# Half products in two bank tiles, with the last product's matmuls between them, and weight differences in later slots

## The chip, the cores and the metric

One core of a Trainium2 chip. The metric is the device time of one execution in microseconds (us); the kernel before takes 1305.6 us in the median of three runs.

## What is computed

Three parts in a chain, all in fp32. The attention is local: chunks of 32 queries with a window of 16 keys to the left and 8 to the right and 8 memory keys, for 4 batches, 8 heads, 768 tokens, head size 64. Then two feed-forward parts over 3072 tokens of width 512:

```python
x = attention(q, k, v, mem_k, mem_v)          # 3072 x 512
h = x @ w_in                                  # 512 x 2048
x = np.where(h > 0, h, np.exp(np.minimum(h, 0)) - 1) @ w_out
a = x @ w1                                    # 512 x 1024
b = x @ w2
out = ((a * b) @ w3) @ w_out2                 # 1024 x 1024, 1024 x 512
```

## The kernel before

Every fp32 operand of a matmul is split into a high and a low part (`split`, `hi_of` and `lo_of`: a cast on ScalarE, a subtraction on VectorE), and a product is three matmuls: high by high, high by low, low by high (`mm3`, and lines 661 to 663 of `mm_half`). The weights come as 64-bit numbers and are put together by `rebase`, `shift` and `low`.

The order of the work is written out by hand: each engine runs its instructions in the order in which the Python code emits them, and a dependency tracker adds the waits. It tracks PSUM and SBUF by tile.

**The middle stage** (the loop over `n` at line 746, blocks of 384 tokens, 16 steps a block). A step runs `mm_h` (12 matmuls, x @ w_in), the activation on ScalarE and VectorE (`elu_exp`, `elu_max` on line 545, `elu_hi` on line 549, `elu_lo` on line 553), and `mm_x` of two steps earlier (12 matmuls with w_out). Between these, `at_step` runs small pieces of other work twice a step, taken from a table of slots that line 500 fills: the attention of the block that comes next, one group of 128 tokens at a time, and the preparation of the second feed-forward part's weights. A `Duo` takes one column block of w1 and w2, forms differences of its parts for the products of the last stage, splits them and stores them to DRAM: `duo_plain`, `duo_first`, `duo_second` and `duo_last`, each into a tile of the pool `st`, which has two buffers. `duo_second` has three subtractions on VectorE (lines 459 to 461, all recorded as line 443) before its cast (line 438) and its last subtraction (line 439). There are eight Duos, two a block in four blocks. `at_out` (slot 8; lines 120 and 121) reads the attention's result out of the PSUM tile `PA`, called `banks` in the trace; `mid_flip` (slot 9) transposes a w3 block into the same tile (line 419) and splits it from there (lines 172 and 175). `store_next` starts the stores of finished tiles at the beginning of each slot.

**The last stage** (the loop at line 848, 32 steps: four pairs of 384-token blocks, times 8 column blocks f of the second part). `mm_ab` computes the columns of a and b for both blocks of a pair in a seven-product scheme of Strassen's kind: seven half products of six matmuls with 384 columns. They alternate between the two banks y and z of `PA`:

```python
    def mm_ab(n):
        y, z = PA[:, 0, 0:TB], PA[:, 1, 0:TB]
```

After a half product ScalarE copies the bank out (lines 669, 673, 675) or VectorE adds it to an earlier result (line 443); the last two give a * b for the two blocks (c11 * c12 and y * c22), which are split into `gq`. Then `left_step` prepares an operand for the next pair, SP issues the loads of weights for step n + 3 (`load_wq`, four loads, 1.8 MB), and `mm_o(n - 1)` multiplies the step before with the folded weights of w3 @ w_out2: 18 matmuls of 512 columns into six accumulators, `PS[0]` to `PS[5]`. Each eighth step is followed by `store_out`, six copies (lines 115 and 117) and six stores.

Of the kernel before, what the change touches and what calls it, by code (L numbers as in the profile page):

```python
# [8 lines left out]
F32 = mybir.dt.float32  # L9
# [10 lines left out]
def tile_kernel(  # L20
# [23 lines left out]
    nc = tc.nc  # L44
    P = 128
# [11 lines left out]
    KT = DM // P  # L57
    NT = B * S
    TB = 384
    NB = NT // TB  # L60
    GPB = TB // GQ
    FF1 = w_in.shape[1] // P
    FF2 = w1.shape[1] // P
# [12 lines left out]
    f_p = ctx.enter_context(tc.tile_pool(name="f_p", bufs=4))  # L76
# [7 lines left out]
    PA = psum.tile([P, 2, 512], F32, name="banks")  # L84
    PS = [None if i < KT else psum.tile([P, 512], F32, name=f"bank{i}") for i in range(6)]
# [27 lines left out]
    def copy_on(eng, o, i):  # L113
        if eng == "a":
            nc.scalar.copy(o, i)
        else:
            nc.vector.tensor_copy(o, i)

    def split(hi, lo, src):
        nc.scalar.copy(hi, src)  # L120
        nc.vector.tensor_tensor(out=lo, in0=src, in1=hi.bitcast(F32), op=ALU.subtract)  # L121

    def mm3(o, w_hi, w_lo, x_hi, x_lo, start, stop):
        mm(o, lhsT=w_hi, rhs=x_hi, start=start, stop=False)  # L124
        mm(o, lhsT=w_hi, rhs=x_lo, start=False, stop=False)  # L125
        mm(o, lhsT=w_lo, rhs=x_hi, start=False, stop=stop)  # L126
# [60 lines left out]
    class Feed:  # L187
# [11 lines left out]
        def do(self, i, *ops):  # L199
            if 0 <= i < len(self.jobs):  # L200
                for op in ops:
                    op(self.jobs[i])
# [239 lines left out]
    def sub(o, a, b, op=ALU.subtract):  # L442
        nc.vector.tensor_tensor(out=o, in0=a, in1=b, op=op)  # L443
        return o
# [39 lines left out]
    def put(at, fn, arg):  # L484
        slots.setdefault(int(at), []).append((at, len(slots.get(int(at), ())), fn, arg))

    def base(G):
        return 2 * FF1 * (G - GPB) // GPB + 1, "slow"
# [6 lines left out]
    def plan(s0, job, *steps):  # L495
        mid_jobs.append(job)
        for at, fn in steps:
            put(s0 + at, fn, job)

    for G in range(GPB, NG):  # L500
        s0, pace = base(G)
        for at, fn in zip(paces[pace], chain):
            put(s0 + at, fn, G)
        if G < GM:
            continue
        if G % GPB and duos:
            duo = duos.pop(0)
            plan(s0, duo.jobs[0], (0, rebase), (1, mid_low))
            plan(s0, duo.jobs[1], (2, rebase), (3, mid_low))
            for at, fn in ((2, duo_plain), (6, duo_first), (7, duo_second), (8, duo_last)):  # L510
                put(s0 + at, fn, duo)
        elif wos:
            plan(s0, wos.pop(0), (0, rebase), (1, mid_low), (2, mid_split))
        if w3s and (not G % GPB or len(duos) % 4 < 3):
            plan(s0, w3s.pop(0), (4, rebase), (5, mid_low), (9, mid_flip))
# [101 lines left out]
    def load_wq(n, parts=range(4)):  # L617
        if n < NPAIR * FF2:
            for r in parts:
                nc.sync.dma_start(out=wq[n % FOLD][r].bitcast(F32), in_=wqd[n % FF2][r])  # L620

    NPAIR = NB // 2
    PLACE = dict(b11=(0, 0), b21=(0, 1), t1=(1, 0), t3=(1, 1), t2=(2, 0), t4=(2, 1), b22=(3, 0))

    def right(n, what):
        r, h = PLACE[what]
        return [wq[n % FOLD][r][:, i, h * 256:(h + 1) * 256] for i in range(2)]
# [5 lines left out]
    def load_x1(p):  # L633
        for r in range(2):
            for k in range(2):
                t = late.tile([P, 2, TB], F32, tag=f"x1{r}{k}", name="x1")
                nc.sync.dma_start(out=t, in_=x1d[2 * p + r][:, 2 * k:2 * k + 2, :])
                x1_t[p, r, k] = t

    def left_step(p, i):  # L640
        a11, a12, a21, a22 = (x1_t[p, r, k] for r in range(2) for k in range(2))
        if i == 3:
            x1_t[p, "s1"] = sub(late.tile([P, 2, TB], F32, tag="s1", name="s1"), a21, a22, ALU.add)
        s1 = x1_t.get((p, "s1"))
        if i == 4:
            sub(a21, a11, a21)
            sub(a11, s1, a11)
        if i == 6:
            sub(a12, a12, a11)
        src = (a11, a12, a22, s1, a11, a21, a12)[i]  # L650
        hi, lo = left[p % 2][LEFTS[i]]
        split(hi, lo, src)

    e_f, gq = {}, []

    def mm_half(n, o, x, w, start, more):
        xs, ws = left[n // FF2 % 2][x], right(n, w)
        for i in range(2):
            c = slice(i * P, (i + 1) * P)
            args = ws[0][:, c], ws[1][:, c], xs[0][:, i, :], xs[1][:, i, :]  # L660
            mm(o, lhsT=args[0], rhs=args[2], start=start and i == 0, stop=False, skip_group_check=more)  # L661
            mm(o, lhsT=args[0], rhs=args[3], start=False, stop=False, skip_group_check=more)  # L662
            mm(o, lhsT=args[1], rhs=args[2], start=False, stop=i == 1, skip_group_check=more)  # L663

    def mm_ab(n):
        y, z = PA[:, 0, 0:TB], PA[:, 1, 0:TB]
        r1, r2, r5, c11, c12, c22 = (e_f[i] for i in range(6))
        mm_half(n, y, "a11", "b11", True, True)
        nc.scalar.copy(r1, y)
        mm_half(n, z, "a12", "b21", True, True)  # L670
        sub(c11, z, r1, ALU.add)
        mm_half(n, y, "s2", "t2", False, True)
        nc.scalar.copy(r2, y)
        mm_half(n, z, "s1", "t1", True, True)
        nc.scalar.copy(r5, z)
        mm_half(n, y, "s3", "t3", False, True)
        sub(c22, y, r5, ALU.add)
        mm_half(n, z, "s4", "b22", False, True)
        sub(c12, z, r2, ALU.add)
        mm_half(n, y, "a22", "t4", False, True)  # L680
        sub(c11, c11, c12, ALU.mult)
        sub(c22, y, c22, ALU.mult)
        for r, e in enumerate((c11, c22)):
            nc.scalar.copy(gq[2 * (n % 2) + r][:, 0, :], e)  # L684
        for r, e in enumerate((c11, c22)):
            g = gq[2 * (n % 2) + r]
            sub(g[:, 1, :], e, g[:, 0, :].bitcast(F32))

    def mm_o(n):
        f = n % FF2  # L690
        w = W[s_wc[f]]
        for t in range(2 * TB // P):
            g = gq[2 * (n % 2) + t // GPB]
            c = slice(t % GPB * P, (t % GPB + 1) * P)
            mm3(PS[t], g[:, 0, c], g[:, 1, c], w[:, 0, :], w[:, 1, :], f == 0, f == FF2 - 1)

    def store_out(p):
        for t in range(2 * TB // P):
            o = f_p.tile([P, 512], F32, tag="f", name="st")
            copy_on("av"[t % 2], o, PS[t])  # L700
            r0 = 2 * p * TB + t * P
            nc.sync.dma_start(out=out[r0:r0 + P, :], in_=o)


    with tc.manual_schedule():
# [40 lines left out]
        for n in range(NH + 2):  # L746
            j, f, at, last = seq[n] if n < NH else (NB, n - NH, n - NH, False)
# [99 lines left out]
        NA = NPAIR * FF2  # L847
        for n in range(NA + 1):
            p, f = divmod(n, FF2)
            if n < NA:  # L850
                mm_ab(n)
                if p + 1 < NPAIR and f >= 1:
                    left_step(p + 1, f - 1)
                if p + 2 < NPAIR and f == FF2 - 1:
                    load_x1(p + 2)
                load_wq(n + FOLD)
            if n >= 1:
                mm_o(n - 1)
                if f == 0:
                    store_out(p - 1)  # L860


# [28 lines left out]
```

## Time and profile before

| | |
|---|---|
| median of three runs | 1305.6 us (1304.9 to 1306.8) |
| profiled execution: its own time | 1306.04 us |
| its span in the trace | 1304.1 us |
| mean granted TensorE clock | 0.98 of full |
| attention and middle stage | up to some 710 us |
| weight products (w3 @ w_out2) | some 708 to 754 us |
| last stage | some 754 to 1300 us |

Engines in the profile: PE is TensorE's matmuls, PEld its weight loads, DVE VectorE, ACT ScalarE, SP the engine that issues nearly all DMAs. A row of the view in order of time gives the start, the duration, engine, line, operation, output <- inputs and, in brackets, how long the engine stood idle before it and who released it. The ends of matmuls are modelled, and they overlap: the pace is read from their starts.

### The profile page before, as it was taken

How to read it: one execution, taken by the hardware profiler on the slowest of the kernel's cores; microseconds unless marked ns; L12 is line 12 of the kernel's file. 1: busy time of each engine (PE TensorE's matmuls, PEld its weight loads, DVE VectorE, ACT ScalarE, POOL GpSimd, SP SyncE). 2: the span in 40 equal slices, each digit the busy share in tenths (PEclk: the TensorE clock that was granted, in tenths of full speed). 3: DMA queues.
4: the chain of work that ended last, by engine and by line, in shares of the span. 5: the costliest groups of instructions: out<-in, count | busy, mean ns of one | idle time of the engine just before them, and what ended most of it. 6: DMA issues, size and time to landing. Idle time of an engine off the chain costs nothing.

```text
span 1304.1 us, 20830 instructions
## 1 busy us (share of the span) xinstructions
PE 1113.8 (85%) x8528; PEld 991.5 (76%) x8528; DVE 596.9 (46%) x1080; ACT 463.1 (36%) x965; POOL 1.7 (0%) x16
## 2 busy tenths in 40 slices
PE   4788998998989989999999977777777777777777
PEld 3788998988989889999999756666666666665665
DVE  4898565665665656654524132233233322322222
ACT  3676454544544545445433121112111211111111
POOL 0000000000000000000000000000000000000000
PEclk9889998998999989999999999999999999999999
DMA  8855554554445545342276343326333543334311
GB/s 205 246 149 130 157 155 152 151 155 160 128 155 150 173 153 152 106 135 69 85 270 195 129 131 112 108 86 226 113 104 106 194 129 112 100 103 161 101 37 49
DMA packets 170090, 180.40 MB, mean 138 GB/s; under 512 B 101388, under 2 KB 140300, under 8 KB 169996
## 3 DMA queue, kind: packets, MB, share of 16 engines
q1 hardware_dynamic: 168956, 178.81, 44.5%
q8 instruction: 67, 1.10, 0.4%
q10 hardware_dynamic: 1040, 0.26, 0.1%
q14 instruction: 27, 0.22, 0.1%
HBM read 139.20 MB, written 39.85 MB: 137 GB/s over the span
## 4 chain that ended last, share of the span: by engine, by line
PE 53%; DVE 22%; ACT 16%; issue 5%; DMA 3%; DVEq 0%; ACTq 0%; SPq 0%
PE banks L661 10%; PE bank L124 9%; PE bank L125 9%; PE bank L126 9%; PE banks L663 6%; PE banks L662 6%; DVE e L443 4%; ACT g L549 3%; DVE eg L545 2%; DVE pT L377 2%; DVE e L366 2%; DVE f L167 1%; DVE g L553 1%; DVE f L163 1%; ACT eg L540 1%
## 5 line engine op out<-in xcount | busy, mean ns | idle before, releaser
L124 PE MATMUL bank<-xhl,w 128*128 128x384 f32 x512 | 179.5, 351 | 13.1 <-DVE eg L545 12.2
L124 PE MATMUL bank<-g,w 128*128 128x384 f32 x512 | 178.8, 349 | 0.0
L125 PE MATMUL bank<-g,w 128*128 128x384 f32 x512 | 174.7, 341 | 0.0
L126 PE MATMUL bank<-g,w 128*128 128x384 f32 x512 | 174.6, 341 | 0.0
L125 PE MATMUL bank<-xhl,w 128*128 128x384 f32 x512 | 173.6, 339 | 0.9 <-DVE xhl L121 0.9
L126 PE MATMUL bank<-xhl,w 128*128 128x384 f32 x512 | 173.5, 339 | 0.0
L661 PE MATMUL banks<-xd,w 128*128 128x384 f32 x224 | 85.7, 383 | 63.2 <-DVE e L443 33.2
L443 DVE TENSOR_TENSOR e<-banks,e 128x384 f32<-128x384 f32 x64 | 35.7, 558 | 195.8 <-PE banks L663 195.8
L549 ACT CAST g<-eg 128x384 fp32r<-128x384 f32 x128 | 66.0, 516 | 160.5 <-DVE eg L545 160.5
L553 DVE TENSOR_TENSOR g<-eg,g 128x384 fp32r<-128x384 f32 x128 | 71.4, 558 | 97.1 <-ACT g L549 97.1
L661 PEld LDWEIGHTS banks<-xd,w 128*128 128x128 f32 x224 | 41.9, 187 | 94.8 <-DVE e L443 48.8
L124 PEld LDWEIGHTS bank<-xhl,w 128*128 128x128 f32 x512 | 97.7, 191 | 20.4 <-DVE eg L545 17.1
L443 DVE TENSOR_TENSOR e<-banks,eg 128x384 f32<-128x384 f32 x64 | 35.7, 558 | 159.9 <-PE banks L663 159.9
L124 PEld LDWEIGHTS bank<-g,w 128*128 128x128 f32 x512 | 98.9, 193 | 1.1
L125 PEld LDWEIGHTS bank<-g,w 128*128 128x128 f32 x512 | 98.8, 193 | 0.2 <-DVE g L553 0.2
L125 PEld LDWEIGHTS bank<-xhl,w 128*128 128x128 f32 x512 | 97.9, 191 | 1.3 <-DVE xhl L121 1.3
L126 PEld LDWEIGHTS bank<-g,w 128*128 128x128 f32 x512 | 98.7, 193 | 0.0
L126 PEld LDWEIGHTS bank<-xhl,w 128*128 128x128 f32 x512 | 97.8, 191 | 0.0
L545 DVE SCALAR_TENSOR_TENSOR eg<-eg,bank 128x384 f32<-128x384 f32 x128 | 69.8, 545 | 60.4 <-ACT eg L540 60.4
L684 ACT CAST g<-e 128x384 fp32r<-128x384 f32 x64 | 32.9, 513 | 175.8 <-DVE e L443 175.8
L539 ACT ACTIVATE eg<-bank 128x384 f32<-128x384 f32 x128 | 62.5, 489 | 61.5 <-PE bank L126 61.5
L663 PE MATMUL banks<-xd,w 128*128 128x384 f32 x224 | 75.6, 338 | 0.0
(135 smaller groups left out, 1910.9 us busy)
## 6 DMA issues: line engine op xcount, KB each, us to landing
w<-wqd SPq DMA_DIRECT2D x96, 512.0 KB
raw<-in_moe_w_dram SPq DMA_DIRECT2D x32, 512.0 KB
wqd<-st SPq DMA_DIRECT2D x24, 512.0 KB
raw<-in_moe_w_out_dram SPq DMA_DIRECT2D x20, 512.0 KB
w3d<-st SPq DMA_DIRECT2D x16, 512.0 KB
w<-w3d SPq DMA_DIRECT2D x16, 512.0 KB
w<-wqd SPq DMA_DIRECT2D x32, 256.0 KB
raw<-in_moe_w_in_dram SPq DMA_DIRECT2D x12, 512.0 KB
```

The source lines that it names most:

```text
L124: mm(o, lhsT=w_hi, rhs=x_hi, start=start, stop=False)
L125: mm(o, lhsT=w_hi, rhs=x_lo, start=False, stop=False)
L126: mm(o, lhsT=w_lo, rhs=x_hi, start=False, stop=stop)
L443: nc.vector.tensor_tensor(out=o, in0=a, in1=b, op=op)
L539: nc.scalar.activation(e, h_t[n], AF.Relu, scale=-1.0)
L545: nc.vector.scalar_tensor_tensor(out=e, in0=e, scalar=-1.0, in1=h_t.pop(n), op0=ALU.add, op1=ALU.max)
L549: nc.scalar.copy(g_t[n][:, 0, :], eg_t[n])
L553: nc.vector.tensor_tensor(out=g[:, 1, :], in0=eg_t.pop(n), in1=g[:, 0, :].bitcast(F32), op=ALU.subtract)
L661: mm(o, lhsT=args[0], rhs=args[2], start=start and i == 0, stop=False, skip_group_check=more)
L662: mm(o, lhsT=args[0], rhs=args[3], start=False, stop=False, skip_group_check=more)
L663: mm(o, lhsT=args[1], rhs=args[2], start=False, stop=i == 1, skip_group_check=more)
L684: nc.scalar.copy(gq[2 * (n % 2) + r][:, 0, :], e)
```

## The change

Half products go into `PS[4]` and `PS[5]`, two tiles of one bank each. The last product's accumulators five and six go into the two halves of `PA`, which is one tile. The 18 matmuls of the last product no longer follow the step as a block: they stand in six groups of three between its half products, after the second, third, fourth and fifth (one group each) and after the seventh (two). `left_step` is issued ahead of the first group, and the copy and the store of an accumulator directly behind its group. In the middle stage the slots of the weight differences change: `duo_first` from 6 to 7, `duo_last` from 8 (ahead of what the group of attention does later) to 8.5, `duo_second` from 7 to 9.5.

```diff
-            for at, fn in ((2, duo_plain), (6, duo_first), (7, duo_second), (8, duo_last)):
+            for at, fn in ((2, duo_plain), (7, duo_first), (8.5, duo_last), (9.5, duo_second)):
...
+    def acc(t):
+        return PS[t] if t < KT else PA[:, t - KT, :]
+
+    def mm_step(n, last, between):
+
+        y, z = PS[4][:, 0:TB], PS[5][:, 0:TB]
+        if last:
+            for i in sorted(between):
+                between[i]()
+            return
         r1, r2, r5, c11, c12, c22 = (e_f[i] for i in range(6))
+        do = lambda i: between[i]() if i in between else None
         mm_half(n, y, "a11", "b11", True, True)
         nc.scalar.copy(r1, y)
         mm_half(n, z, "a12", "b21", True, True)
         sub(c11, z, r1, ALU.add)
+        do(0)
         mm_half(n, y, "s2", "t2", False, True)
         nc.scalar.copy(r2, y)
+        do(1)
         mm_half(n, z, "s1", "t1", True, True)
         nc.scalar.copy(r5, z)
+        do(2)
         mm_half(n, y, "s3", "t3", False, True)
         sub(c22, y, r5, ALU.add)
+        do(3)
         mm_half(n, z, "s4", "b22", False, True)
         sub(c12, z, r2, ALU.add)
         mm_half(n, y, "a22", "t4", False, True)
+        do(4)
+        do(5)
         sub(c11, c11, c12, ALU.mult)
         sub(c22, y, c22, ALU.mult)
...
+    def mm_o(n, t):
...
+    def store_out(p, t):
...
         for n in range(NA + 1):
             p, f = divmod(n, FF2)
+
+            def behind(t, n=n, p=p, f=f):
+                if t == 0 and n < NA and p + 1 < NPAIR and f >= 1:
+                    left_step(p + 1, f - 1)
+                if n >= 1:
+                    mm_o(n - 1, t)
+                    if f == 0:
+                        store_out(p - 1, t)
+
+            mm_step(n, n == NA, {t: lambda t=t: behind(t) for t in range(2 * GPB)})
             if n < NA:
...
                 load_wq(n + FOLD)
-            if n >= 1:
-                mm_o(n - 1)
-                if f == 0:
-                    store_out(p - 1)
```

What the change does to the issue order, at three places. First PE, in the second step of the last stage, about the second half product; `banks` is the tile `PA`, `bank_95` and `bank_96` are `PS[4]` and `PS[5]`, `bank_606` is `PS[0]`, and what a row waits for stands in brackets. Before, the first half, the second half and the start of the third:

```order
L661 MATMUL banks<-xhl_73,w_77 128x384
L662 MATMUL banks<-xhl_73,w_77 128x384
L663 MATMUL banks<-xhl_73,w_77 128x384
L661 MATMUL banks<-xhl_73,w_77 128x384 [waits Activation_49]
L662 MATMUL banks<-xhl_73,w_77 128x384
L663 MATMUL banks<-xhl_73,w_77 128x384
L661 MATMUL banks<-xhl_73,w_77 128x384
L662 MATMUL banks<-xhl_73,w_77 128x384
L663 MATMUL banks<-xhl_73,w_77 128x384
L661 MATMUL banks<-xc_7195,w_79 128x384 [waits DMAHW6_49,DVE_49]
```

And now, from the end of the second half on:

```order
L663 MATMUL bank_96<-xhl_73,w_77 128x384
L661 MATMUL bank_96<-xhl_73,w_77 128x384
L662 MATMUL bank_96<-xhl_73,w_77 128x384
L663 MATMUL bank_96<-xhl_73,w_77 128x384
L124 MATMUL bank_606<-w_76,g 128x512 [waits Activation_49]
L125 MATMUL bank_606<-w_76,g 128x512
L126 MATMUL bank_606<-w_76,g 128x512 [waits DVE_49]
L661 MATMUL bank_95<-xc_7195,w_79 128x384 [waits DMAHW6_49,Activation_49]
L662 MATMUL bank_95<-xc_7195,w_79 128x384
```

The second half has lost its wait for ScalarE (Activation); the last product's first group stands between the second and the third half, and the third half waits for ScalarE, which reads the first.

Second, VectorE in the middle stage, in the last group of attention of a block with weight differences; line 377 belongs to the attention, 443 and 439 to the weight differences (`duo_first`, then `duo_second`, and a single 439 of `duo_last`), 545 and 553 to the activation, 121 to `at_out`, 175 to `mid_flip`. Before:

```order
L377 STREAM_TRANSPOSE pT<-e_3386 128x1024
L443 TENSOR_TENSOR st<-f 128x256 x2
L439 TENSOR_TENSOR st<-st 128x512
L443 TENSOR_TENSOR st<-f 128x256
L443 TENSOR_TENSOR st<-st,f 128x256
L443 TENSOR_TENSOR st<-f,st 128x256
L439 TENSOR_TENSOR st<-st 128x512
L545 SCALAR_TENSOR_TENSOR eg<-eg,bank_95 128x384
L553 TENSOR_TENSOR g<-eg,g 128x384
L121 TENSOR_TENSOR xhl_74<-banks,xhl_74 128x2x4x64
L439 TENSOR_TENSOR st<-f,st 128x256
L175 TENSOR_TENSOR st<-banks,st 128x512
```

And now:

```order
L377 STREAM_TRANSPOSE pT<-e_3386 128x1024
L443 TENSOR_TENSOR st<-f 128x256 x2
L439 TENSOR_TENSOR st<-st 128x512
L545 SCALAR_TENSOR_TENSOR eg<-eg,bank_95 128x384
L553 TENSOR_TENSOR g<-eg,g 128x384
L121 TENSOR_TENSOR xhl_74<-banks,xhl_74 128x2x4x64
L439 TENSOR_TENSOR st<-f,st 128x256
L175 TENSOR_TENSOR st<-banks,st 128x512
L443 TENSOR_TENSOR st<-f 128x256
L443 TENSOR_TENSOR st<-st,f 128x256
L443 TENSOR_TENSOR st<-f,st 128x256
L439 TENSOR_TENSOR st<-st 128x512
```

The four rows of `duo_second` have gone from ahead of the activation and of line 121 to behind line 175, where they stand ahead of the next activation.

Third, VectorE at the end of a step that stores (the ninth step of the last stage). Before, with the two products, their two subtractions and the three copies:

```order
L443 TENSOR_TENSOR e_8036<-banks,eg 128x384 [waits PE_49]
L443 TENSOR_TENSOR e_8035<-e_8035,e_8036 128x384 [waits DVE_49]
L443 TENSOR_TENSOR e_8037<-banks,e_8037 128x384 [waits PE_49]
L443 TENSOR_TENSOR g<-e_8035,g 128x384 [waits Activation_49]
L443 TENSOR_TENSOR g<-e_8037,g 128x384 [waits Activation_49]
L117 COPY st<-bank_607 128x512 [waits DMAHW7_49,PE_49]
L117 COPY st<-bank_609 128x512 [waits DMAHW1_49,PE_49]
L117 COPY st<-bank_96 128x512 [waits DMAHW7_49,DVE_49,PE_49]
```

And now:

```order
L117 COPY st<-bank_609 128x512 [waits DMAHW5_49,PE_49]
L443 TENSOR_TENSOR e_8036<-bank_96,eg 128x384 [waits PE_49]
L117 COPY st<-banks 128x512 [waits DVE_49,DMAHW3_49,PE_49,Activation_49]
L443 TENSOR_TENSOR e_8035<-e_8035,e_8036 128x384 [waits DVE_49]
L443 TENSOR_TENSOR e_8037<-bank_95,e_8037 128x384
L443 TENSOR_TENSOR g<-e_8035,g 128x384 [waits Activation_49]
L443 TENSOR_TENSOR g<-e_8037,g 128x384 [waits Activation_49]
```

The copy of the sixth accumulator now stands ahead of the two products, and waits for ScalarE as well, which reads the fifth accumulator in the same tile.

## Rows read from the trace of the kernel before

**Rows 1.** The page, first part: busy time of the engines, share, instructions.
```profile
PE 1113.8 (85%) x8528; PEld 991.5 (76%) x8528; DVE 596.9 (46%) x1080; ACT 463.1 (36%) x965; POOL 1.7 (0%) x16
```

**Rows 2.** Busy time by stretch: end of the middle stage, last stage (x: instructions).
```profile
core 0: us, PE busy (x) PEld busy (x) DVE busy (x) ACT busy (x) POOL busy (x), PEclk, DMA share, GB/s
648.00:708.50 60.50, 60.50 (x351) 60.50 (x350) 18.62 (x33) 23.99 (x47) 0.00 (x0) 1.00 0.70 230
754.40:1300.40 546.00, 419.71 (x1922) 333.48 (x1920) 161.87 (x271) 102.45 (x195) 0.00 (x0) 1.00 0.35 114
```

**Rows 3.** The waits: engine, tile, line <- releaser: us in total, times, longest.
```profile
PE banks L661 <- DVE e L443: 66.4, 96, 0.7
...
PE banks L661 <- ACT eg L669: 21.1, 32, 1.0
...
PE banks L419 <- DVE xhl L121: 20.9, 6, 4.2
```

**Rows 4.** In order of time: PE in two steps of the last stage.
```profile
1103.90 0.34 PE L662 MATMUL banks<-xhl,w 128*128 128x384 f32 x1
...
1104.77 0.39 PE L124 MATMUL bank<-w,g 128*128 128x512 f32 x1
...
1108.89 0.33 PE L661 MATMUL banks<-xhl,w 128*128 128x384 f32 x1
...
1109.77 0.34 PE L663 MATMUL banks<-xhl,w 128*128 128x384 f32 x1
...
1110.74 0.44 PE L661 MATMUL banks<-xhl,w 128*128 128x384 f32 x1 [0.62 <-ACT eg L669]
...
1125.88 0.33 PE L661 MATMUL banks<-xhl,w 128*128 128x384 f32 x1
```

**Rows 5.** In order of time: ACT and DVE in the same stretch.
```profile
1110.20 0.48 ACT L669 COPY eg<-banks 128x384 f32<-128x384 f32 x1 [1.81 <-PE banks L663]
...
1119.99 0.56 DVE L443 TENSOR_TENSOR e<-banks,eg 128x384 f32<-128x384 f32 x1 [1.42 <-PE banks L663]
...
1122.43 1.22 DVE L443 TENSOR_TENSOR g<-e,g 128x384 fp32r<-128x384 f32 x2
...
1124.55 0.96 DVE L443 TENSOR_TENSOR x<-s,x 128x768 f32<-128x768 f32 x1
...
1125.55 0.83 ACT L120 CAST xd<-x 128x768 fp32r<-128x768 f32 x1 [2.49 <-DVE x L443]
```

**Rows 6.** In order of time: DVE's and ACT's copies in a storing step.
```profile
901.88 0.68 DVE L117 COPY st<-bank 128x512 f32<-128x512 f32 x1
...
905.39 0.58 ACT L115 COPY st<-bank 128x512 f32<-128x512 f32 x1 [2.46 <-DMA out_dram<-st]
```

**Rows 7.** In order of time: PE in the middle stage, about two waiting transposes.
```profile
271.35 0.66 PE L419 MATMUL banks<-ident,f 128*128 128x128 f32 x4 [1.99 <-DVE xhl L121]
...
298.09 0.34 PE L126 MATMUL bank<-g,w 128*128 128x384 f32 x1
302.66 1.11 PE L419 MATMUL banks<-ident,f 128*128 128x128 f32 x4 [4.24 <-DVE xhl L121]
...
303.90 0.52 PE L125 MATMUL bank<-g,w 128*128 128x384 f32 x1
304.22 0.52 PE L126 MATMUL bank<-g,w 128*128 128x384 f32 x1
...
311.35 0.42 PE L124 MATMUL bank<-g,w 128*128 128x384 f32 x1
```

**Rows 8.** In order of time: DVE ahead of the second of these.
```profile
296.74 0.42 DVE L443 TENSOR_TENSOR st<-f 128x256 f32<-128x256 f32 x1
...
299.37 0.55 DVE L545 SCALAR_TENSOR_TENSOR eg<-eg,bank 128x384 f32<-128x384 f32 x1
...
301.92 0.69 DVE L121 TENSOR_TENSOR xhl<-banks,xhl 128x512 fp32r<-128x512 f32 x1 [0.86 <-ACT xhl L120]
```

**Rows 9.** The chain that ended last: start, duration, a store in the middle stage.
```profile
266.49 4.81 DMA wqd<-st
```

More of the change, by code (lines that the diff above doesn't have):

```diff
@@ L663, in mm_half @@
             mm(o, lhsT=args[1], rhs=args[2], start=False, stop=i == 1, skip_group_check=more)
-    def mm_ab(n):
-        y, z = PA[:, 0, 0:TB], PA[:, 1, 0:TB]
+    def acc(t):
[6 more added lines that the diff above has]
+            return
         r1, r2, r5, c11, c12, c22 = (e_f[i] for i in range(6))
+        do = lambda i: between[i]() if i in between else None
         mm_half(n, y, "a11", "b11", True, True)
@@ L687, in mm_ab @@
             sub(g[:, 1, :], e, g[:, 0, :].bitcast(F32))
-    def mm_o(n):
+    def mm_o(n, t):
         f = n % FF2
         w = W[s_wc[f]]
[L692 to L702, printed above, removed]
+        g = gq[2 * (n % 2) + t // GPB]
+        c = slice(t % GPB * P, (t % GPB + 1) * P)
+        mm3(acc(t), g[:, 0, c], g[:, 1, c], w[:, 0, :], w[:, 1, :], f == 0, f == FF2 - 1)
+    def store_out(p, t):
+        o = f_p.tile([P, 512], F32, tag="f", name="st")
+        copy_on("av"[t % 2], o, acc(t))
+        r0 = 2 * p * TB + t * P
+        nc.sync.dma_start(out=out[r0:r0 + P, :], in_=o)
     with tc.manual_schedule():
@@ L849, in tile_kernel @@
             p, f = divmod(n, FF2)
+            def behind(t, n=n, p=p, f=f):
[6 more added lines that the diff above has]
+            mm_step(n, n == NA, {t: lambda t=t: behind(t) for t in range(2 * GPB)})
             if n < NA:
-                mm_ab(n)
-                if p + 1 < NPAIR and f >= 1:
-                    left_step(p + 1, f - 1)
                 if p + 2 < NPAIR and f == FF2 - 1:
```

## The prediction

> **What bounds the kernel now.** I read the views in this order: busy time by engine, busy time by stretch, the waits, the instructions in order of time, and the issue order of both kernels. By the first, TensorE (PE) is busy 85% of the span and every other engine under half [rows 1]; so PE, or what holds PE up, sets the time. By stretch, PE is full at the end of the middle stage (60.5 us busy of 60.5), and has its largest hole in the last stage, 754.4 to 1300.4 us: 419.7 us busy of 546.0, at granted clock 1.00 [rows 2]. A 126 us hole there is a lower bound, because the modelled ends of pipelined matmuls count as busy. The waits name it: PE's matmuls of line 661 wait for VectorE (DVE) at line 443 96 times and for ScalarE (ACT) at line 669 32 times, about 0.7 us each [rows 3]. These are the half products, whose two banks lie in one tile: each half waits until the half before it, in the other bank, has been read.
>
> The order of time gives the size. A step starts at 1108.89 and the next at 1125.88: 16.99 us. Inside a half, five starts take 0.87 us (1103.90 to 1104.77), 0.174 each; the 18 matmuls of 512 columns take 4.12 us (1104.77 to 1108.89), 0.229 each. So the 42 + 18 matmuls of a step need 7.31 + 4.12 = 11.43 us, and 5.56 us are six gaps of 0.93. One gap: the last start of a half at 1109.77, the copy out at 1110.20, the next half at 1110.74 [rows 4, 5].
>
> A second hole lies in the middle stage, by the same waits: the transposes of line 419 wait six times, 20.9 us, for DVE's line 121 [rows 3].
>
> **Last stage, the gaps.** Reading a bank costs PE 0.43 us from the last start to the reader, 0.48 (ACT) or 0.56 (DVE) for the reader, and 0.06 to the next start: 0.97 or 1.05 us [rows 4, 5]. In the new order a half need only wait for the half before it in its own bank, and the issue order shows just those waits left. In between stand another half (1.05) and one or two groups of the last product (0.69 each). From the last start of a half to the first start of the next one in its bank that makes 1.91 us after the first and the fifth half (1.05 + 0.69 + 0.174) and 2.6 us or more after the second, third, fourth and sixth, against 1.05 needed. The tightest is from the seventh half to the next step's first: only groups five and six, 2 x 0.69 + 0.174 = 1.55 us. There DVE has three instructions of 0.56 in a row: the sum after the sixth half ends about 0.06 before the seventh half's last start, the first product 0.50 after it, the second 1.06 after it; with 0.06 the bank is free at 1.12. That fits by 0.4 us, so all six gaps close: 32 steps x 5.56 = **177.9 us gained**.
>
> What lies behind these waits now? The last product's first group needs the result of the step before: cast (about ACT's 0.48) and subtraction (1.22 for two) end about 1.7 and 2.3 us after the seventh half, while PE comes to it after 1.55 + 2.1. The input splits move in front of ACT's second copy; the worst one has two subtractions of 0.96 and a cast of 0.83 in the way [rows 5]: counted from the second half's last start 0.43 + 0.56 + 1.92 + 0.83 + 0.48 + 0.06 = 4.28 us, where the fifth half wants its bank at 4.34. It costs nothing, by 0.06 us, in the three steps that have it. The 1.8 MB of weights per step are issued when a step's last halves free their buffers, and are wanted two steps later: over 20 us for 160 GB/s, where 230 GB/s ran in a stretch in which PE was full [rows 2]. In a step that stores, the weights stand behind six stores on SP's queue and are issued some 3 us later; two steps still cover that.
>
> **New waits.** Accumulators five and six now share the tile with two banks. In the steps that store (three, and the end) group six waits for ACT's copy out of group five: 0.43 + 0.58 + 0.06 instead of 0.229, so 0.84 us. Then DVE copies accumulator six (0.68) ahead of the two products, and the next step's first half waits for these: 0.43 + 0.68 + 0.56 + 0.56 + 0.06 instead of 0.229, so 2.06 us [rows 5, 6]. With slower first starts 3.0 us, three times: 9.0. The end pays 0.84 and about 0.15 because the last result is covered by two groups, not six: 1.0. The buffers' own wait for the stores (2.46 us before ACT's fifth copy [rows 6]) is gone, as the copies now stand 1.7 us apart. Last stage: 177.9 - 10.0 = **167.9 us**; bounds 145 (0.7 us per step not closed) and 169 (no new wait at all but the end's).
>
> **Middle stage.** Four transposes wait 4.2 us, like that at 302.66 (PE's last start before it 298.09), two 2.0 us, like that at 271.35. After the long wait the transposes take 1.11 us in place of 0.66 and matmuls 0.52 in place of 0.34: PE is on its lower clock level for some 12 of them [rows 7]. DVE's row shows the cause: the three subtractions that start at 296.74 and the cast and subtraction behind them run until 299.37, 2.63 us, ahead of the instruction that frees the bank (301.92) [rows 8]. The change puts these 2.63 us behind the transposes; so the bank is free at 300.0 instead of 302.6, the wait is 1.6 us, and without the lower clock PE would be at its row of 311.35 at about 306.4. But the moved work then stands ahead of the activation of that step, and its two staging buffers are not free: it needs the buffer of the short store issued at about 300.4. A store of twice the size took 4.81 us [rows 9]; so the buffer is free between 302.8 and 305.2, the moved work ends 2.6 us later, and the activation's three instructions 1.8 us after that: 307.2 to 309.6, when PE goes on. Gain 1.7 to 4.1 us; if the clock falls again, 2.3 less. I take 2.4, nearer to the late end because the wait moves rather than goes: 4 x 2.4 = 9.6. Of the two 2.0 us waits I take 1.7 each (bounds 0 and 2): 3.4. Together **13 us**, bounds -2 and +20. The groups without a wait now gain and lose nothing: their DVE work only changes places under a full PE.
>
> **Sum.** Against the profiled execution's own 1306.0 us (span 1304.1; 0.4 above the median of 1305.6): 1306.0 - 167.9 - 13 = **1125 us**.
>
> **Rivals.**
> - One reuse in each step does not fit. For: the slack at the step's end is only 0.4 us and rests on three DVE rows back to back. Price one gap a step, 32 x 0.93 = 30 us: 1155 us. Against: all distances but that one are nearly twice the need or more.
> - Loads set the pace. For: a step asks for 160 GB/s where the last stage moved 114 GB/s. If 115 GB/s were the most this stage can get, a step took 1.835 MB / 115 GB/s = 16.0 us; 32 x 1.0 us and the middle's 13 gained: 1261 us. It decides below 160 GB/s. Against: 230 GB/s beside a full PE [rows 2].
> - The change does not separate the halves, only the middle gains: 1293 us. Against: the issue order no longer has the second half's wait for ACT.
> - Slower. PE on its lower clock through the last stage: starts 0.32 us apart in place of 0.174, as behind the wait at 302.66 [rows 7], all 365.8 us of matmuls times 1.84 = 673, so 546 becomes 683 with the new waits, less 13: 1430 us. It decides from 60% of the stage on the lower level. For: no stretch of this kernel is full for 370 us. Against: clock 1.00 in every full stretch [rows 2]; it fell only after waits [rows 7].
>
> [...] In this trace the releasers of the half products are DVE and ACT, not a DMA [rows 3].
>
> **Chances.** Forecast 0.80 (its own range 1112 to 1140: the middle's bounds and some unclosed slack), one reuse misfit or the middle worse by over 10 us 0.12, loads 0.03, not separated 0.02, slower 0.02, else 0.01. The range 1110 to 1148 holds the forecast and the nearer part of the second case. A difference under 0.2% could not be measured; nearly every case is far from it: faster 0.97, same 0.01, slower 0.02.
>
> **What would show it.** Right: steps of 11.4 us; no wait of line 661's matmuls for DVE or ACT except at the three storing steps, each about 3 us; four waits of line 124 for line 115 of about 0.8 us; line 419's waits under 2 us, with new waits of line 124 for line 553 or 545 in the middle. Wrong: waits of half products in each step, waits for w tiles' DMAs, a granted clock under 1.00 in the last stage, or a middle stage as long as before.

## The result, and the profile after

The changed kernel takes **1132.4 us** in the median of four runs (1131.9 to 1133.0), against 1305.3 us for the kernel before on the same chip: a ratio of 0.868 (95% interval 0.866 to 0.869). One run of experiment 1 (1699 us) and one of experiment 2 (2640 us) lay far above all others of the same kernel and are left out of the times below. The prediction was 1125 us with a range of 1110 to 1148: right in sign, cause and range, 7 us too low.

The page's first part, after, answers to [rows 1]: 1062.1 us of work in a span of 1131.1.

```profile
PE 1062.1 (94%) x8528; PEld 996.0 (88%) x8528; DVE 593.2 (52%) x1080; ACT 461.3 (41%) x965; POOL 1.7 (0%) x16
```

Busy time by stretch, after: the last stage (the second row of [rows 2]; x is the number of instructions), and in it an ordinary step, a storing step and the step behind that.

```profile
core 0: us, PE busy (x) PEld busy (x) DVE busy (x) ACT busy (x) POOL busy (x), PEclk, DMA share, GB/s
742.30:1127.50 385.20, 376.36 (x1921) 347.43 (x1920) 157.83 (x271) 100.39 (x195) 0.00 (x0) 0.99 0.50 163
...
773.80:785.30 11.50, 11.50 (x61) 10.74 (x60) 4.54 (x9) 3.15 (x6) 0.00 (x0) 1.00 0.49 160
831.50:846.00 14.50, 12.03 (x61) 10.48 (x60) 5.25 (x10) 3.67 (x8) 0.00 (x0) 0.98 0.52 198
846.00:860.40 14.40, 14.38 (x60) 13.47 (x61) 5.04 (x9) 3.66 (x8) 0.00 (x0) 0.79 0.65 220
```

The stage shrank from 546.0 to 385.2 us, and PE is full in the ordinary step. The third step has no hole either (14.38 busy of 14.40), yet it is 2.9 us too long: its granted clock is 0.79. That is what the prediction did not have. The loads now move 163 GB/s beside it, as the prediction reckoned (160).

The waits, after, in the order of [rows 3]. The waits of half products in every step are gone. Of the two new kinds, line 661 waits for line 443 at the three storing steps (1.77 us each) and once, 0.7 us, at the stage's start, and line 124 for line 115 at the three storing steps and at the end.

```profile
PE banks L419 <- DVE xhl L121: 6.4, 4, 1.6
...
PE bank L661 <- DVE e L443: 6.0, 4, 1.8
...
PE banks L305 <- ACT memo L300: 5.5, 3, 2.2
...
PE banks L124 <- ACT st L115: 2.9, 4, 0.7
...
PE bank L124 <- ACT g L549: 2.8, 2, 1.6
```

In order of time, PE from a storing step's group five on; against [rows 4], where starts inside a half lie 0.17 us apart.

```profile
842.18 0.40 PE L126 MATMUL banks<-w,g 128*128 128x512 f32 x1
843.29 0.51 PE L124 MATMUL banks<-w,g 128*128 128x512 f32 x1 [0.72 <-ACT st L115]
...
843.86 0.39 PE L126 MATMUL banks<-w,g 128*128 128x512 f32 x1
846.02 0.69 PE L661 MATMUL bank<-xd,w 128*128 128x384 f32 x1 [1.77 <-DVE e L443]
846.51 0.52 PE L662 MATMUL bank<-xd,w 128*128 128x384 f32 x1
846.83 0.52 PE L663 MATMUL bank<-xd,w 128*128 128x384 f32 x1
```

DVE in the same stretch:

```profile
844.34 0.69 DVE L117 COPY st<-banks 128x512 f32<-128x512 f32 x1 [2.91 <-PE banks L126]
844.95 0.55 DVE L443 TENSOR_TENSOR e<-e,e 128x384 f32<-128x384 f32 x1
845.41 0.55 DVE L443 TENSOR_TENSOR e<-bank,e 128x384 f32<-128x384 f32 x1
```

The two waits stand where the prediction put them: group six starts 1.11 us after the last start of group five (predicted 0.43 + 0.58 + 0.06 = 1.07), and the next half 2.16 us after the last start of group six (predicted 2.29), behind one copy and two products on DVE. Behind them matmuls of 384 columns start 0.32 us apart and take 0.52, which are the numbers of the lower clock level in [rows 7].

The middle, after. PE about a transpose of line 419 in the second block, and about the first transposes of the attention's next group (line 305):

```profile
294.57 0.34 PE L126 MATMUL bank<-g,w 128*128 128x384 f32 x1
296.49 0.65 PE L419 MATMUL banks<-ident,f 128*128 128x128 f32 x4 [1.59 <-DVE xhl L121]
...
303.46 0.66 PE L305 MATMUL banks<-ident,qn 128*128 128x128 f32 x4 [1.59 <-ACT memo L300]
...
304.31 0.42 PE L124 MATMUL bank<-g,w 128*128 128x384 f32 x1
```

DVE and then ACT there:

```profile
299.45 0.43 DVE L443 TENSOR_TENSOR st<-f 128x256 f32<-128x256 f32 x1 [0.96 <-DMA wqd<-st]
...
302.14 0.55 DVE L545 SCALAR_TENSOR_TENSOR eg<-eg,bank 128x384 f32<-128x384 f32 x1
```

```profile
302.72 0.51 ACT L549 CAST g<-eg 128x384 fp32r<-128x384 f32 x1 [1.22 <-DVE eg L545]
303.14 0.18 ACT L299 COPY front<-banks 128x32 f32<-128x32 f32 x1
303.21 0.19 ACT L300 COPY memo<-banks 128x32 f32<-128x32 f32 x1
```

Line 419 now waits 1.59 us (4.24 before [rows 7]), and its matmuls run at the higher level (0.65). The moved `duo_second` waits 0.96 us for its staging buffer and stands ahead of the activation: DVE comes to line 545 only at 302.14. ACT's cast (line 549) waits for it, and behind that cast stand the two small copies out of PSUM that line 305 waits for: 1.59 us. The matmul that stood at 311.35 before stands at 304.31, and the last one ahead of the transposes at 294.57 where it stood at 298.09 [rows 7]: of 7.04 us, 3.52 had been gained before this place and 3.52 are gained here. The fourth block waits in the same way, 2.17 us, and there PE comes down to its lower level:

```profile
472.51 0.66 PE L305 MATMUL banks<-ident,qn 128*128 128x128 f32 x4 [2.17 <-ACT memo L300]
...
473.93 0.52 PE L125 MATMUL bank<-g,w 128*128 128x384 f32 x1
474.25 0.52 PE L126 MATMUL bank<-g,w 128*128 128x384 f32 x1
```

The two waits of 2.0 us at line 419 are gone, but two shorter ones have come behind each of them, in which PE waits for DVE's line 545; before, neither of these matmuls waited. Behind the first:

```profile
283.78 0.44 PE L124 MATMUL bank<-xhl,w 128*128 128x384 f32 x1 [0.66 <-DVE eg L545]
...
289.02 0.45 PE L124 MATMUL bank<-xhl,w 128*128 128x384 f32 x1 [0.80 <-DVE eg L545]
```

### The profile page after: what moved, and what is told of

Same layout as the page of the kernel before. It is cut to its first block, busy times and chain, and to the rows that moved or that the text cites. A ratio compares the mean times of both kernels' runs of the same rounds, so it can differ in the third digit from the quotient of the medians.

```text
span 1131.1 us, 20839 instructions
## 1 busy us (share of the span) xinstructions
PE 1062.1 (94%) x8528; PEld 996.0 (88%) x8528; DVE 593.2 (52%) x1080; ACT 461.3 (41%) x965; POOL 1.7 (0%) x16
## 4 chain that ended last, share of the span: by engine, by line
PE 62%; DVE 18%; ACT 13%; issue 4%; DMA 3%; DVEq 0%; SPq 0%; ACTq 0%
PE bank L124 11%; PE bank L125 11%; PE bank L126 11%; PE bank L661 7%; PE bank L662 7%; PE bank L663 7%; ACT g L549 3%; DVE eg L545 3%; PE banks L124 2%; DVE e L366 2%; PE banks L126 2%; PE banks L125 2%; DVE pT L377 1%; DVE g L553 1%; ACT eg L540 1%
## 5 line engine op out<-in xcount | busy, mean ns | idle before, releaser
L124 PE MATMUL bank<-g,w 128*128 128x384 f32 x512 | 176.0, 344 | 2.8 <-ACT g L549 2.8
L125 PE MATMUL bank<-g,w 128*128 128x384 f32 x512 | 172.1, 336 | 0.3 <-DVE g L553 0.3
L126 PE MATMUL bank<-g,w 128*128 128x384 f32 x512 | 172.0, 336 | 0.0
L124 PEld LDWEIGHTS bank<-g,w 128*128 128x128 f32 x512 | 96.7, 189 | 4.4 <-ACT g L549 3.2
L125 PEld LDWEIGHTS bank<-g,w 128*128 128x128 f32 x512 | 96.8, 189 | 1.0 <-DVE g L553 1.0
L126 PEld LDWEIGHTS bank<-g,w 128*128 128x128 f32 x512 | 96.5, 189 | 0.0
L443 DVE TENSOR_TENSOR e<-bank,e 128x384 f32<-128x384 f32 x64 | 35.4, 554 | 104.9 <-PE bank L663 61.5
L443 DVE TENSOR_TENSOR e<-bank,eg 128x384 f32<-128x384 f32 x64 | 35.7, 558 | 91.8 <-PE bank L663 91.8
L661 PE MATMUL bank<-xd,w 128*128 128x384 f32 x224 | 76.1, 340 | 3.5 <-DVE e L443 3.5
L662 PE MATMUL bank<-xd,w 128*128 128x384 f32 x224 | 76.7, 342 | 0.0
L663 PE MATMUL bank<-xd,w 128*128 128x384 f32 x224 | 76.4, 341 | 0.0
```

## The experiments

Two theories on the last stage stood at the start. By the one each half waited only because its neighbour's bank lay in the same tile, so the separation alone closes the gaps. By the other it is the groups' work that covers a bank's reading, so the separation alone leaves part of each gap. And two questions: what do the slots give, and what costs the 7 us that the prediction lacks? Where an expectation calls theories by letters, they are those of its own experiment.

**1. The new slots alone**, in the kernel before.

```diff
-            for at, fn in ((2, duo_plain), (6, duo_first), (7, duo_second), (8, duo_last)):
+            for at, fn in ((2, duo_plain), (7, duo_first), (8.5, duo_last), (9.5, duo_second)):
```

> The kernel before with the new slots of the weight differences alone. Theory (the two parts add up, and the middle stage gives the 12.2 us by which the last stage starts earlier in the changed kernel: 754.58 to 742.35): 1305.3 - 12.2 = 1293 us, the last stage's steps still 17.0 us. Rival (the middle gains only together with the last stage, or by chance of the trace): 1305 us.

Measured: 1298.1 us in the median of four runs against 1305.5, ratio 0.994 (0.991 to 0.997), so 4 to 12 us gained. The single times fall in two groups, 1293.4 and 1294.7, 1301.6 and 1301.6: the first is the theory's number, the second is nearer to the rival's. The profiled execution is the 1293.4 one. Its stretch up to the first half product:

```profile
130.00:742.00 612.00, 589.51 (x5428) 558.92 (x5427) 332.75 (x621) 284.16 (x610) 0.00 (x0) 1.00 0.50 152
```

The same stretch of the kernel before, up to its first half product:

```profile
130.00:754.50 624.50, 598.27 (x5432) 568.98 (x5431) 333.05 (x621) 284.57 (x610) 0.00 (x0) 0.98 0.49 150
```

It is 12.5 us shorter, of which 8.8 us are PE's busy time (598.3 to 589.5) for the same matmuls, at clock 1.00 against 0.98. So most of what this execution gained is clock and not waiting: before, the level fell behind each of the four waits of 4.2 us. The other group has no profile, and the mean granted clock of the whole run does not sort the two: 0.995 and 0.987 in the first, 0.979 and 0.988 in the second. What parts them stays open.

**2. The last stage alone**: the changed kernel with the old slots (experiment 1's diff, reversed).

> The changed kernel with the old slots of the weight differences. Theory (parts add): 1132.4 + 12.2 = 1144.6 us, with the four waits of 4.2 us and the two of 2.0 us at line 419 back and steps of 11.55 us in the last stage. Rival: 1132 us.

Measured: 1139.9 us (1139.8 to 1139.9), ratio 0.873 (0.872 to 0.875). The slots are worth 1139.9 - 1132.4 = 7.5 us on top of the last stage, and 1305.5 x 0.0059 = 7.7 without it. By the totals the parts add; the middle's term was 13. The expectation was 4.7 us too high, and the two profiled executions show why: the last stage starts at 752.04 (754.58 in the kernel before, by the same code up to there), 9.7 us later than in the changed kernel, and is then 2.9 us shorter than there, because the steps behind the storing ones took 13.12, 11.66 and 11.66 us in place of 14.43, 13.23 and 11.66. Line 419's waits are back:

```profile
PE banks L419 <- DVE xhl L121: 20.9, 6, 4.2
```

**3. The separation alone**: the 18 matmuls as one block behind the step again, with `left_step` and the stores where they were.

```diff
-            mm_step(n, n == NA, {t: lambda t=t: behind(t) for t in range(2 * GPB)})
+            if n < NA:
+                mm_step(n, False, {})
+                if p + 1 < NPAIR and f >= 1:
+                    left_step(p + 1, f - 1)
             if n < NA:
...
                 load_wq(n + FOLD)
+            if n >= 1:
+                for t in range(2 * GPB):
+                    mm_o(n - 1, t)
+                if f == 0:
+                    for t in range(2 * GPB):
+                        store_out(p - 1, t)
```

> The changed kernel with the last product's 18 matmuls as one block behind the step, and the input splits and the copies behind it, as before; the two tiles for the halves stay. Theory A (the tile was the whole cause; one half of 1.05 + 0.17 = 1.22 us between two uses of a bank covers the 0.97 or 1.05 us that reading it takes): steps of about 11.5 us and no 2.9 us in the storing steps, so 1132.4 - 3 x 2.9 - 4.6 (the two steps after a storing one that ran on the lower clock) - 0.9 = 1118 us. Theory B (one half is too short a cover, because the weight load of the next half has to start before its first matmul; the groups in between are needed): 0.1 to 0.3 us at five reuses, steps of 12 to 13 us, 1135 to 1165 us.

Measured: 1131.0 us (1129.6 to 1131.3), ratio 0.866 (0.865 to 0.868), which cannot be told apart from the whole change. On the gaps the first theory is right: ordinary steps take 11.43 to 11.51 us, and no half product waits in them. One other half (1.05 us, 1.22 from the last start before it to the first behind it) is enough cover for a turnaround of 0.97 to 1.05. But the time is what neither theory gave, because three steps take 16.7, 17.2 and 12.7: the ones behind the storing steps, whose copies and stores now stand at their end. In order of time in the first of them, ACT:

```profile
849.28 0.58 ACT L115 COPY st<-banks 128x512 f32<-128x512 f32 x1 [6.19 <-DMA out_dram<-st]
849.76 0.48 ACT L678 COPY eg<-bank 128x384 f32<-128x384 f32 x1
```

and PE:

```profile
850.30 0.69 PE L661 MATMUL bank<-xd,w 128*128 128x384 f32 x1 [3.69 <-ACT eg L678]
850.79 0.52 PE L662 MATMUL bank<-xd,w 128*128 128x384 f32 x1
```

ACT's copy of accumulator five waits for a staging buffer that a store still reads, the copy of the next step's first half is queued behind it, PE waits 3.7 us for that, and the clock falls. The groups between the halves thus buy one thing here: they space the six copies so that the buffers are free.

**4. The groups alone**: y and z both in `PA` again, the accumulators `PS[0]` to `PS[5]`.

```diff
-        return PS[t] if t < KT else PA[:, t - KT, :]
+        return PS[t]
...
-        y, z = PS[4][:, 0:TB], PS[5][:, 0:TB]
+        y, z = PA[:, 0, 0:TB], PA[:, 1, 0:TB]
```

> The changed kernel with both halves' banks in the one tile again (and the accumulators in six tiles of their own); the six groups stay between the halves. Theory (a group of 0.69 us covers its part of a gap and no more): the gaps after the first and the sixth half stay at 0.9 to 1.0 us, the four with one group shrink to 0.2 to 0.3: about 2.9 us a step over 11.55, so 14.4 us a step, and 1132.4 + 32 x 2.9 - 3 = 1222 us. Rival 1 (the groups do most of the work, not the tiles): under 1170 us. Rival 2 (they do nothing): about 1290 us.

Measured: 1220.5 us (1219.8 to 1222.2), ratio 0.935 (0.933 to 0.936), with ordinary steps of 14.23: half of the gain, as expected. The waits show which gaps stay, those with no group in them:

```profile
PE banks L661 <- DVE e L443: 27.3, 37, 1.7
...
PE banks L661 <- ACT eg L678: 19.7, 32, 0.6
```

**5. The last two copies later**: the changed kernel with the copies and stores of accumulators five and six behind the step's products and splits.

```diff
-                    if f == 0:
+                    if f == 0 and t < 4:
                         store_out(p - 1, t)
 
             mm_step(n, n == NA, {t: lambda t=t: behind(t) for t in range(2 * GPB)})
+            if n >= 1 and f == 0:
+                for t in (4, 5):
+                    store_out(p - 1, t)
```

> The changed kernel with one thing moved: in a storing step the copies of accumulators five and six stand behind the step's two products and their splits, so group six does not wait for ACT's copy and the products do not wait for DVE's. Theory: three times 2.9 us go, the lower clock in the steps behind (2.9 and 1.7 us in the changed kernel's trace) goes with them since no wait is left to bring it, and the end's 0.9: 1132.4 - 8.7 - 4.6 - 0.9 = 1118 us. Rival 1 (the lower clock has another cause than these waits): 1123 us, with a step of 13 to 14.5 us still behind a storing one. Rival 2 (the moved copies hold up ACT's first copy of the next step or the buffers of the stores): 1125 us or more.

Measured: 1120.3 us (1119.5 to 1120.6), ratio 0.858 (0.857 to 0.860): between the theory's number and the first rival's, and the steps decide for the theory. From the third on every step takes 11.55 us, storing or not, and those behind the storing ones too, where that rival wanted 13 to 14.5; one wait of a half product is left, at the stage's start:

```profile
PE bank L661 <- DVE e L443: 0.7, 1, 0.7
```

12.1 us come from taking away two waits in each of three steps: 3 x 2.92 = 8.8 in the storing steps and 4.7 in the steps behind, 13.5 by the two traces. The steps behind lost their 4.7 us together with the waits, so these were the waits' doing. How much they cost differs from execution to execution: 4.7 in the change, 1.8 in experiment 2 with the same waits.

**6. One of the two waits**: the copy of accumulator five moved behind group six, both copies still ahead of the products.

```diff
-                        store_out(p - 1, t)
+                        for u in ((t,), (), (4, 5))[max(0, t - 3)]:
+                            store_out(p - 1, u)
```

> The changed kernel with the copy of accumulator five moved behind group six, but both copies still ahead of the products: the 0.72 us wait of group six goes (three times and at the end), the wait of 1.77 us before the next step's first half stays. Theory (the lower clock needs both waits close together: 1.6 to 2.2 us alone did not bring it in the middle stage): 1132.4 - 4 x 0.9 - 4.6 = 1124 us. Rival (the wait of 1.77 us alone brings it): 1129 us, with slow matmuls still behind one or two storing steps.

Measured: 1129.9 us (1128.9 to 1132.5), ratio 0.866 (0.865 to 0.867): the rival's number, but by another road. Group six no longer waits, and the next half's wait, which both had left at 1.77 us, grew:

```profile
847.02 0.44 PE L661 MATMUL bank<-xd,w 128*128 128x384 f32 x1 [2.38 <-DVE e L443]
847.30 0.33 PE L662 MATMUL bank<-xd,w 128*128 128x384 f32 x1
```

Storing steps took 14.09. The steps behind took 11.66, 13.20 and 11.68: one wait of 2.4 us brought the lower clock once in three times. The theory took waits of 1.6 to 2.2 us in the middle stage not to have brought it; but in the changed kernel it fell behind the wait of 2.17 us at 472.51. Much of a wait that is taken away at one place of a chain can come back at the next: 0.72 us went, 0.61 came.

**7. No weight loads** in the last stage after the first three steps, against the 0.12 us by which an ordinary step (11.55) is longer than predicted (11.43).

```diff
-                load_wq(n + FOLD)
```

> The changed kernel without the loads of weights behind the first three steps: later steps multiply with the weights of an earlier column block, so this part of the computation is left out. Asked is why a step takes 11.55 us and not the 11.43 worked out from the rows of before. Theory A (the denser loads, some 170 GB/s where before it was 114, slow the matmuls' reads a little): steps of 11.43 us, 1132.4 - 32 x 0.12 = 1128.5 us. Theory B (the alternation of groups itself, or the readers of the banks beside it, costs 0.12 us a step): steps of 11.55, 1132 us.

Measured, in one run: 1133.5 us, ordinary steps still 11.55. The loads are not the cause; the storing steps were 14.47 as in the change, those behind 13.21, 11.69 and 14.38.

**8. A block behind the step, and the last two copies in the next step**: experiment 3 with accumulators five and six copied out behind the fourth and the fifth half of the step that follows.

```diff
-                mm_step(n, False, {})
+                mm_step(n, False, {t - 2: lambda t=t: store_out(p - 1, t) for t in (4, 5)} if f == 1 and n > 1 else {})
...
-                    for t in range(2 * GPB):
+                    for t in range(4 if n < NA else 6):
                         store_out(p - 1, t)
```

> The kernel with the split alone (last product as a block behind the step), with one thing moved: the copies and stores of accumulators five and six stand in the next step, behind its fourth and fifth half, so that the wait for the stores' buffers is no longer ahead of ACT's first copy. Theory (that wait of 3.7, 3.9 and 1.0 us at the first copy and the lower clock behind it were all that the split alone lost): every step at its 11.42 to 11.52 us, 1131.0 - (5.2 + 5.7 + 1.3) = 1118.5 us, some 2 us under the kernel with the groups in between and late copies (1120.3), whose steps take 11.55. Rival (the groups are what covers the copies; without them others wait): 1122 us or more.

Measured: 1118.0 us (1117.8 to 1118.1), ratio 0.856 (0.854 to 0.858), as expected. From the third on all steps take 11.43 to 11.51. So with the stores out of the way the six groups between the halves are not needed.

**9. `duo_second` later still** (slot 10.5), on top of experiment 8.

```diff
-            for at, fn in ((2, duo_plain), (7, duo_first), (8.5, duo_last), (9.5, duo_second)):
+            for at, fn in ((2, duo_plain), (7, duo_first), (8.5, duo_last), (10.5, duo_second)):
```

> As the kernel of the run before in this call, with duo_second another slot later (10.5). Theory (in the changed kernel's middle stage the waits that took the place of the old ones, two of 1.1 to 2.0 us at line 549 and two of 1.6 to 3.1 us at line 300, come from duo_second standing ahead of the activation; one slot later it stands behind it): 6 to 9 us less, 1110 to 1112 us, those four waits gone, the 1.6 us waits at line 121 unchanged. Rival (the work waits for its staging buffer wherever it stands, and only moves the wait on to the next activation): within 2 us of the run before.

Measured: **1113.7 us** (1112.5 to 1114.1), ratio 0.852 (0.850 to 0.854), the best kernel of this study, 1.7% below the change. The expected time was a little lower, since part of the wait only moved on. Its waits:

```profile
PE bank L124 <- DVE eg L545: 20.7, 19, 3.1
...
PE banks L305 <- ACT memo L300: 1.7, 1, 1.7
```

Experiment 8's:

```profile
PE bank L124 <- DVE eg L545: 15.4, 15, 3.1
...
PE banks L305 <- ACT memo L300: 6.4, 3, 3.2
...
PE bank L124 <- ACT g L549: 3.2, 2, 2.1
```

7.9 us of waits for ACT went, 5.3 us of waits for DVE's line 545 came; the last stage starts 4.0 us earlier (739.59 against 743.62). In the last stage the trace now shows next to no idle time, and what waiting is left lies in front of it:

```profile
739.50:1108.00 368.50, 367.74 (x1922) 343.15 (x1920) 158.68 (x271) 100.83 (x195) 0.00 (x0) 1.00 0.52 170
```

## Why the prediction was right, and where it was off

In the two profiled executions the last stage went from 545.6 us (first half product's start to the last matmul's) to 385.0, each with that matmul's 0.229: 160.6 gained where 167.9 was predicted. From the matmuls alone (365.8 us by the prediction's starts) the stage is 19.2 us away: 31 steps x 0.12 = 3.8, storing steps 8.8, steps behind them 4.7, and about 1 each at the start and the end. The prediction had 10.0 of these; and the steps before had 1.9 us more than 32 x 16.99, which it did not count and which went too. That is the last stage's miss: 19.2 - 10.0 - 1.9 = 7.3. Its upper bound in the prediction, 169, is a slip: no new wait but the end's would be 177.9 - 1.0 = 176.9.

- **The gaps (177.9): right.** The releasers were found right, the turnaround was right, and all six gaps closed. Experiments 3 and 4 name the cause: the separation closes all of them, the groups alone half. The tightest distance, at the step's end, was reckoned to fit by 0.4 us; no ordinary step waits there.
- **The ordinary step: mis-sized.** "So the 42 + 18 matmuls of a step need 7.31 + 4.12 = 11.43 us" took the starts of unmixed rows. With groups between the halves a step takes 11.55, in all four pairs; with the block behind the step it takes 11.51 in the first and third pair and 11.43 in the others. So the groups in turn cost 0.04 us in half of the steps and 0.12 in the others, and the block itself 0.08 more in one half than in the other. The difference of 3.8 us over the stage has no wait in it and is not the loads' (experiment 7); its cause stays open.
- **The new waits (10.0): right in place and size.** A storing step took 14.47, 2.92 more than others, where 3.0 was predicted; the end's share is too small to be judged apart.
- **The clock behind these waits: left out.** The prediction wrote "with slower first starts 3.0 us, three times" and gave the lower level no more than that, though its own [rows 7] showed the level fall behind a wait. The steps behind the storing ones lost 2.88, 1.68 and 0.11 us: 4.7. Experiment 5 shows that they go when the waits go.
- **The middle (13): a sum near the profiled one, by terms that were not.** The waits of line 419 became 1.6 us as predicted. The delay by the staging buffer came too, 0.96 us in the second block, and so did the wait for the late activation. But the prediction named line 124 as the one that waits, and that is so in the first and third block (1.63 and 1.14 us); in the second and fourth it is line 305, through two ACT copies queued behind the late cast (1.59 and 2.17 us). That ACT queue was not followed. Up to the last stage PE's matmuls are the same in both kernels and in the same order, so their starts can be set against each other one by one. By them the four long waits gave 3.0, 3.5, 2.5 and 2.4 us, where 2.4 each was taken. The two waits of 2.0 us gave 0.4 each, where 1.7 each was taken: 2.2 us are gained at the transposes and 1.8 lost again at the next two activations, because DVE is no sooner done with its line 545 there (0.66 and 0.80 us of waiting at 283.78 and 289.02). Together 12.2 us by these two executions, and 7.5 by the medians of experiment 2. One execution does not size this term to the microsecond: with the new slots the last stage starts between 742.2 and 744.3 in the eight profiled kernels that have them, with the old ones at 752.0 and 754.6, so 8 to 12 us.
- **The rivals.** A reuse that doesn't fit would show a wait of line 661 in each step: there is none. Loads: 163 GB/s moved beside a full PE, with no wait for a weight tile. No separation: the waits are gone. The lower clock throughout: 0.99 over the stage. The Trainium skill ("TensorE: Matmul & The Clock Gate", section "HAM oscillation — how this bites in real kernels") reports that PSUM double-buffering gave no further gain in a matmul kernel whose loop had been rebuilt against the DMA waits that let its clock fall. In this case the measurement decides, and it went the other way: the half products waited for the reader of a neighbouring bank, and separate tiles, with the new slots, took 174 us away (experiment 3).

## What to carry to other kernels

When matmuls wait for the reader of another bank of the same tile, make the banks tiles of their own before reordering anything: here that alone, without the groups in between, gave as much as the whole change, and one neighbouring half of 1.05 us covered a turnaround of 0.97 to 1.05. Then look for what the new owner of the shared tile must wait for; work that can be late (copies and stores of finished results) belongs behind the work that frees a bank, which gave 12 us more. Price a wait on PE with the clock that may fall behind it, and follow the queue of every engine that the late instruction delays, ACT's small copies too.

## What the runs showed of the hardware

- Behind waits of 0.72 and 1.77 us close together, or of 2.38 us alone, PE came down to its lower level in some cases and not in others: the steps behind lost 2.9, 1.7 and 0.1 us in the change, 1.6, 0.1 and 0.1 in experiment 2 with the same waits, 0.1, 1.7 and 0.1 in experiment 6. Behind the two waits of 1.59 us at 296.49 and 303.46 transposes still took 0.65 and 0.66, the higher level's number.
- The length of the wait alone does not decide: at line 305 in the fourth block the level fell behind 2.17 us in the change (matmuls of 0.52 from 473.93 on) but not behind 2.53 us in experiment 1 or 3.16 us in experiment 8 (transposes of 0.66). What decides is open.
- The kernel of experiment 1 kept the higher level through the whole middle stage in its profiled execution (1.00 from 130 to 742 us); its runs lay near 1294 or near 1301.6 us, and why is open.
- Groups of six matmuls with 384 columns and three with 512 in turn cost 0.04 to 0.12 us more a step of 60 than the same matmuls in two blocks (11.55 against 11.51 and 11.43 us), with PE busy throughout.
